# Two head pairs scored in one go, two products with v in one go, and moved buffers, turns and conversions at the two ends of attention

## The chip, the cores and the metric

The kernel runs on one core of a Trainium2 chip. The metric is the time of one execution in microseconds of device time; 561.05 us is the median of three runs of the kernel before (560.88 to 561.12). Engines are named as in the profile: PE is TensorE (PEld its weight loads), DVE is VectorE, ACT is ScalarE, POOL is GpSimd, SP issues most of the DMAs.

## The reference

Three layers follow one another on B = 2 sequences of S = 448 tokens with width C = 768 (12 heads of 64). All is float32.

```python
scores = scale * q @ k.T                      # per head
scores = einsum('bhij,hg->bgij', scores, w_pre)   # heads are mixed before the softmax
attn = softmax(scores, axis=-1)
attn = einsum('bhij,hg->bgij', attn, w_post)      # and after it
x = (attn @ v) as (B, S, 768)
u = x + (relu(x.T @ w_tok1) @ w_tok2).T       # token mixing, 448 -> 256 -> 448
x = u + relu(u @ w_ch1) @ w_ch2               # channel mixing, 768 -> 1536 -> 768
h = gelu(x @ w_in); u, v = halves of h        # 768 -> 2 x 512
v = layernorm(v) * g_ln;  v = w_sg @ v + b_sg # spatial gate over tokens
out = x + (u * v) @ w_out
```

## The kernel before

Nearly every float32 product is computed as three float32r products of split operands (high by high, high by low, low by high); a split is a rounded copy and a subtraction.

**Attention.** A chunk is 120 query rows (88 in the last of a sequence) of all 12 heads; there are eight chunks, four per sequence. `qk` (L345) scores one pair of heads of a chunk: the two heads lie on partitions 0 to 63 and 64 to 127, so each term is two 64-row products into two PSUM banks; two copies bring them to the chunk's tile S. Six pairs make a chunk. A block is 10 query rows by 12 heads, 120 partitions; there are 12 blocks in a full chunk and 9 in a short one, 90 in all. A block's rows are gathered from S by a DMA (`b_dma`, tile P, four buffers in rotation), split by ACT and POOL (`b_high`, `b_low`), mixed over heads and reduced (`b_pre`: three products into a bank of psB, the negated row maximum nm on DVE, the exponential E with its sum on ACT), normalised (`b_norm`: rc, rr on DVE, and wt, the second mixing matrix scaled by the reciprocal sum, on POOL), mixed again and transposed (`b_post`: four products into a bank of psC), and copied to AT by DVE (`b_turn`). `av` (L443) multiplies a finished chunk's AT with v for one pair of heads, in 64-column halves of PE, and copies the result to xT.

The main loop (L544) runs over the steps i from -8 to 89. In step i the DMA of block i+8, the split of i+6, pre of i+4, parts of the normalisation of i+2 and i+1, post of i and the AT copy of i-1 are issued. Every engine works its instructions off in the order written, so this order is the schedule. Extra work hangs on steps: `add(step, fn, ...)` puts it between the normalisation and pre. By it qk of chunk x is spread over the blocks of two chunks before, one pair at a time (L528 to L541), with the splits of the next chunk's q and k (`qprep`, `kprep`: a copy on DVE, a subtraction on POOL) and their loads behind. The products with v of a finished chunk stand in `todo` and are taken one at a time behind post as blocks go by (L575). qk takes two banks of psA, an av one; psA has three banks, psB three, psC two.

**Weights** come as 64-bit floats, and are loaded and converted piece by piece in the order of use: `conv_steps` is a generator, and `pump(n)` takes n calls from it. A piece with a split takes five calls, each of them one DVE instruction or the ACT copy and the subtraction (wl, on POOL for most); `w_abs`, the first step of the next piece (cv, on ACT), is issued at the fourth call; the raw buffers are three, and a finished conversion issues the next load. `rounds(n, w)` advances the evictions that are open and pumps w calls in each of n rounds. Only three converted pieces of the kind in rotation may exist before the first of them is used.

**Behind attention.** `turn` (L462) transposes part of xT back (three PE transposes, then xh on ACT and xl on DVE), since token mixing contracts over tokens: eight turns for the first sequence stand at attention's end, eight for the second within tok1(0), two per group of products. tok1 and tok2 (L653, L673) are the token products; tok2 ends in a chain of an addition on DVE, a copy uh on ACT and a subtraction ul on POOL. The channel products c1 and c2 follow, then the gated layer; there `sps_full(b, d)` (L861) is a quarter of the spatial product of sequence b, followed by the gate's chain (gt twice on DVE, gh on ACT, gl on POOL), and the output products ops read all gates of their sequence.

Of the kernel before, what the change touches and what calls it, by code (L numbers as in the profile page):

```python
# [8 lines left out]
F32 = mybir.dt.float32  # L9
# [10 lines left out]
LD, LS, LP, LN = 8, 6, 4, 2  # L20
NP_BUFS, NPH_BUFS = LD - LS + 2, LS - LP + 1
# [9 lines left out]
def tile_kernel(ctx, tc, q, k, v, w_pre, w_post, w_tok1, w_tok2, w_ch1, w_ch2,  # L31
                w_u, w_v, g_ln, w_sg, b_sg, w_out, out):
    nc = tc.nc
# [63 lines left out]
    def w_dma():  # L97
        i = wstate["dma"]
        if i >= len(pieces):
            return  # L100
        wstate["dma"] += 1
        src, pr, a, n = pieces[i][:4]
        wide = 1 if src.dtype == F32 else 2
        raw = wpool.tile([P, 2 * WC], U32, tag="raw", name=f"raw{i}", bufs=RB)
        r = raw[:pr, :wide * a * n].rearrange("p (a n) -> p a n", a=a)
        nc.sync.dma_start(out=r, in_=src.bitcast(U32))
        wstate["raw"][i] = r
# [64 lines left out]
    def pump(n):  # L172

        for _ in range(n):
            if wstate["conv"] < wstate["room"]:
                next(wstate["steps"], None)
# [107 lines left out]
    def big(nm, dt=F32R):  # L284
        return sp_.tile([P, SWC], dt, tag="S", name=nm, bufs=2)
# [92 lines left out]

    def b_dma(i):
        b, c, j, (r0, stp, m) = blocks[i]  # L380
        t = ap_.tile([BW, S], F32, tag="P", name=f"P{i}", bufs=NP_BUFS)
        nc.sync.dma_start(out=t, in_=SS[b, c][r0:r0 + (m - 1) * stp + 1:stp])
        st[i]["P"] = t

# [39 lines left out]
    def b_post(i):  # L424

        b, c, j, bl = blocks[i]
        if j == 0:
            AT[b, c] = atp.tile([KP, R, H, CH[0][1]], F32, tag="AT", name=f"AT{b}_{c}", bufs=2)
        e, wt = st[i]["e"][0], st[i]["w"]
        ps = psC.tile([P, 512], F32, tag="C", name=f"post{i}")  # L430
        for r in range(R):
            nc.tensor.matmul(ps[:KP, r * BW:(r + 1) * BW], lhsT=e[:, r * KP:(r + 1) * KP], rhs=wt,  # L432
                             start=True, stop=True)
        st[i]["ps"] = ps

    def b_turn(i):

        b, c, j, bl = blocks[i]
        src = st[i]["ps"][:KP, :R * BW].rearrange("p (r g i) -> p r g i", r=R, i=IB)
        nc.vector.tensor_copy(AT[b, c][:, :, :, j * IB:(j + 1) * IB], src)  # L440
        st[i] = None
# [32 lines left out]
    def add(step, fn, *a):  # L474
        extra.setdefault(step, []).append((fn, a))
# [45 lines left out]
    for x in range(2, NCH):  # L521
        b, c = chunks[x]
        n_prev = len(chunk_blocks(CH[chunks[x - 1][1]][1]))
        f0 = first[chunks[x - 1]] - LD
        gap = 3 if n_prev < 12 else 4
        nxt = chunks[x + 1] if x + 1 < NCH else None
        nxt2 = chunks[x + 2] if x + 2 < NCH else None
        for i in range(NP):  # L528
            s_ = f0 + i * n_prev // NP
            LAST = max(LAST, s_)  # L530
            add(s_, qk, b, c, i)
            if nxt and i % QG == QG - 1:
                add(s_ + gap, qprep, *nxt, i // QG)
                if nxt2:
                    add(s_ + gap + 1, load_q, *nxt2, i // QG)
            if nxt and nxt[1] == 0:
                for g, kg in enumerate(KG):
                    if kg[0] == i:
                        add(s_ - 2, load_k, nxt[0], g)

                add(s_ + 2, kprep, nxt[0], i, nc.vector.tensor_copy, nc.gpsimd)  # L541

    todo = []
    for i in range(-LD, NB):  # L544
        if 0 <= i + 1 < NB:
            b_norm(i + 1, 2)
        if i + LD < NB:
            b_dma(i + LD)
        if 0 <= i + LS < NB:
            b_high(i + LS)  # L550
            if i >= 0:
                b_low(i + LS)
        if 0 <= i + LN < NB - (i + LP > NB):
            b_norm(i + LN, 0)
        if i > 0:
            b_turn(i - 1)
        if 0 <= i + LN < NB - (i + LP > NB):
            b_norm(i + LN, 1)
        if i + LP == NB:

            b_norm(NB - 1, 0)
            b_norm(NB - 1, 1)
        for fn, a in extra.get(i, []):
            fn(*a)
        if 0 <= i + LP < NB:
            b_pre(i + LP)
        if -LS <= i < 0:

            b_low(i + LS)
        if i >= 0:  # L570
            b, c, j, bl = blocks[i]
            b_post(i)

            nb = len(chunk_blocks(CH[c][1]))
            while todo and NP - len(todo) < (j + 1) * NP // nb:  # L575
                av(*todo[0])
                if todo[0][1] == len(CH) - 1 and b:
                    add(i + 1, load_v, b, todo[0][2])
                todo.pop(0)
            if j == nb - 1:  # L580
                todo = [(b, c, hp) for hp in range(NP)]
        if i == LAST:
            qctx.close()
            wctx = ctx.enter_context(ExitStack())
            wpool = wctx.enter_context(tc.tile_pool(name="wp", bufs=1, side="right", reuse_waits="tile"))
            tctx = ctx.enter_context(ExitStack())
            tpool = tctx.enter_context(tc.tile_pool(name="tokw", bufs=1, side="right", reuse_waits="tile"))
        if 0 < i - LAST <= 2 * RB and (i - LAST) % 2 == 1:
            w_dma()
        if i + LS + 4 >= NB:  # L590

            pump(1)
    b_turn(NB - 1)

    NS = S // KP
    XR = [big(f"x{nm}0") for nm in "hl"]
    X = {0: [t[:KP, :NS * C].rearrange("p (s c) -> p s c", c=C) for t in XR]}
    RX = {0: [t[:, NS * C:NS * C + TOK // P * C].rearrange("p (t c) -> p t c", c=C) for t in XR]}
    turns = [(0, s, ch) for ch in range(2) for s in range(NS)]

    def turn0(n):
        for _ in range(n):
            turn(psB.tile([P, 512], F32, tag="B", name=f"xps0_{len(turns)}"), *turns.pop(0))

    turn0(3)
    while todo:
        av(*todo.pop(0))
        pump(1)
    turn0(len(turns))
    actx.close()  # L610


# [37 lines left out]
    with ExitStack() as mctx:  # L650
        mp = mctx.enter_context(tc.tile_pool(name="tok", bufs=1, reuse_waits="tile"))
        RR = {}
        def tok1(b, turns=()):  # L653
            xh, xl = X[b]
            t1 = [p for i in p_t1 for p in parts(i)]
            rh, rl = RX[b]
            got = []
            for tt in range(TOK // P):
                ts = slice(tt * P, (tt + 1) * P)
                for ch in range(2):  # L660
                    cs = slice(ch * CW, (ch + 1) * CW)
                    ps = bank(f"t1ps{b}_{tt}_{ch}")
                    mm3(ps[:, :CW], [((t1[s][0][:, ts], t1[s][1][:, ts]), (xh[:, s, cs], xl[:, s, cs]))
                                     for s in range(NS)])
                    got.append(later(relu_split(rh[:, tt, cs], rl[:, tt, cs], ps[:, :CW])))
                    for _ in range(2):
                        if turns:
                            s, tch = turns.pop(0)
                            turn(bank(f"xps1_{s}_{tch}"), 1, s, tch)
                    rounds(2)  # L670
            RR[b] = (rh, rl, got)

        def tok2(b):  # L673
            rh, rl, got = RR[b]
            finish(*got)
            t2 = [p for i in p_t2 for p in parts(i)]
            for cc in range(NCC):
                cs = slice(cc * P, (cc + 1) * P)
                ps = bank(f"t2ps{b}_{cc}")
                mm3(ps[:, :S], [((rh[:, tt, cs], rl[:, tt, cs]), t2[tt]) for tt in range(TOK // P)])  # L680
                U[cc, b] = later(add_split(cc, b, ps[:, :S], uh, ul))
                rounds(1, 1 - b)
                rounds(1, 0)

        X[1] = [mp.tile([KP, NS, C], F32R, name=f"x{nm}1") for nm in "hl"]
        RX[1] = [mp.tile([P, TOK // P, C], F32R, name=f"r{nm}1") for nm in "hl"]
        need(p_t1[-1])

        tok1(0, [(s, ch) for ch in range(2) for s in range(NS)])
        need(p_t2[-1])  # L690
        tok1(1)
        tok2(0)
        tok2(1)
# [167 lines left out]
    def sps_full(b, d):  # L861
        ds = slice(d * P, (d + 1) * P)
        ks = range(MID) if b == 0 else range(MID + 1, NT)
        mm3(banks[b, d][:, :S], [((vh[:, k, ds], vl[:, k, ds]), sg_parts(k, slice(0, P))) for k in ks], start=False)
        G[b, d] = later(gate(b, d, banks[b, d][:, :S]))
        rounds(2)

    finish(*[V[k] for k in range(MID + 1)])
    for d in range(ND - 1):
# [109 lines left out]
```

## Time and profile before

| | |
|---|---|
| median of three runs | 561.05 us |
| the profiled execution's own time | 562.4 us |
| its span in the trace | 560.6 us |
| PE busy | 548.3 us, 98% |
| PEld busy | 476.7 us, 85% |
| DVE busy | 391.6 us, 70% |
| ACT busy | 282.8 us, 50% |
| POOL busy | 282.2 us, 50% |
| granted PE clock, mean of the run | 1.00 |

The busy time of an engine is a union of its instructions' times. PE's products are pipelined: one is shown as running until its last result is out, while the next has begun; what a product costs is therefore read from the distance between two starts and not from its duration. A bracket behind an instruction gives the idle time of its engine before it and what ended it.

### The profile page before, as it was taken

The page shows a single profiled execution, that of the slowest core. Times are in us where ns is not written, and L with a number is a line of the kernel's source. Part 1 is how long each engine was busy: PE and PEld are TensorE (multiplying, and loading weights), DVE is VectorE, ACT ScalarE, POOL GpSimd, SP SyncE. Part 2 cuts the span into 40 slices and gives each one's busy share as a digit, 9 for nine tenths or more (in the row PEclk, how much of TensorE's full clock was granted, in tenths as well). Part 3 has the DMA queues.
Part 4 walks back from the last instruction along what each step waited for, and adds up shares of the span by engine and source line. Part 5 has one row for each costly group of instructions (what it writes and reads, how often), then busy time and mean ns, then how long its engine had stood idle before and what let it go on. Part 6 is the DMA issues. An engine that isn't in the chain of part 4 may idle for free.

```text
span 560.6 us, 10091 instructions
## 1 busy us (share of the span) xinstructions
PE 548.3 (98%) x3630; PEld 476.7 (85%) x3630; DVE 391.6 (70%) x771; ACT 282.8 (50%) x600; POOL 282.2 (50%) x295
## 2 busy tenths in 40 slices
PE   9899999999999999899999999999999999999997
PEld 5677888888888888799789999999999998888786
DVE  4788766555665677778455767678887974795972
ACT  4876776666777665454433344423243343464320
POOL 0599996667666665013922322334544545055610
PEclk9999999999999999999999999999999999999999
DMA  6464534423432362133113443434343323102222
GB/s 203 171 210 136 174 123 99 106 86 121 154 118 87 124 174 50 59 111 115 56 57 94 123 142 112 151 113 151 113 142 121 94 90 111 63 1 68 84 100 98
DMA packets 26340, 63.12 MB, mean 113 GB/s; under 512 B 2914, under 2 KB 18834, under 8 KB 26290
## 3 DMA queue, kind: packets, MB, share of 16 engines
q1 hardware_dynamic: 26002, 62.10, 34.6%
q8 instruction: 29, 0.48, 0.4%
q10 hardware_dynamic: 288, 0.37, 0.2%
q14 instruction: 21, 0.17, 0.1%
HBM read 40.36 MB, written 2.75 MB: 77 GB/s over the span
## 4 chain that ended last, share of the span: by engine, by line
PE 89%; POOL 5%; DVE 3%; ACT 1%; DMA 1%; issue 1%; POOLq 0%; SPq 0%; DVEq 0%; ACTq 0%
PE post L432 13%; PE av L450 7%; PE qk L362 7%; PE c2ps L623 5%; PE c2ps L622 5%; PE c2ps L624 5%; PE c1ps L623 5%; PE c1ps L624 5%; PE pre L399 5%; PE c1ps L622 5%; PE pre L400 3%; PE pre L401 3%; POOL ul L640 3%; PE ups L623 2%; PE ups L624 2%; PE ups L622 2%
## 5 line engine op out<-in xcount | busy, mean ns | idle before, releaser
L393 POOL TENSOR_TENSOR Pl<-P,Ph 120x448 fp32r<-120x448 f32 x87 | 99.5, 1143 | 62.7 <-ACT Ph L387 52.8
L159 POOL TENSOR_TENSOR wl<-cv,wh 128x768 fp32r<-128x768 f32 x28 | 53.0, 1894 | 115.7 <-ACT wh L158 81.2
L432 PEld LDWEIGHTS post<-wt,E 120*112 120x112 f32 x720 | 86.3, 176 | 7.1 <-POOL wt L420 1.7
L432 PE MATMUL post<-wt,E 120*112 120x120 f32 x720 | 88.9, 267 | 1.4 <-POOL wt L420 0.8
L403 DVE TENSOR_REDUCE nm<-pre 120x1 f32<-120x448 f32 x90 | 55.3, 614 | 36.0 <-PE pre L401 35.8
L407 ACT ACTIVATE E<-pre,nm 120x448 f32<-120x448 f32 x90 | 57.3, 636 | 45.3 <-DVE rc L414 31.9
L440 DVE COPY AT<-post 112x480 f32<-112x480 f32 x90 | 58.8, 654 | 7.0 <-PE post L432 0.7
L623 PE MATMUL c1ps<-ul,wh 128*128 128x448 f32 x144 | 53.7, 373 | 1.7 <-POOL ul L640 1.7
L387 ACT CAST Ph<-P 120x448 fp32r<-120x448 f32 x90 | 52.2, 580 | 1.5 <-DMA P<-S 1.5
L623 PE MATMUL c2ps<-r1l,wh 128*128 128x448 f32 x144 | 52.9, 368 | 0.0
L139 DVE SCALAR_TENSOR_TENSOR cv<-raw,cv 128x768 uint32<-128x768 uint32 (+3 forms) x44 | 51.9, 1180 | 1.1
L622 PE MATMUL c1ps<-uh,wh 128*128 128x448 f32 x144 | 52.3, 363 | 0.0
L622 PE MATMUL c2ps<-r1h,wh 128*128 128x448 f32 x144 | 52.3, 363 | 0.0
L624 PE MATMUL c1ps<-uh,wl 128*128 128x448 f32 x144 | 52.0, 361 | 0.0
L624 PE MATMUL c2ps<-r1h,wl 128*128 128x448 f32 x144 | 52.0, 361 | 0.0
L117 ACT ACTIVATE cv<-raw 128x768 f32<-128x768 f32 (+3 forms) x44 | 36.1, 821 | 29.8 <-POOL wl L159 17.6
L365 ACT COPY S<-qk 120x448 f32<-120x448 f32 (+1 forms) x86 | 42.1, 539 | 15.6 <-PE qk L362 13.2
L450 PE MATMUL av<-AT,vn 112*64 112x120 f32 (+1 forms) x768 | 46.5, 266 | 0.4 <-DVE AT L440 0.4
L141 DVE SCALAR_TENSOR_TENSOR cv<-raw,cv 128x768 uint32<-128x768 uint32 (+3 forms) x44 | 42.2, 958 | 1.1
L399 PE MATMUL pre<-Ph,wpl 120*120 120x448 f32 x90 | 40.8, 454 | 1.5 <-DVE rc L414 1.4
L450 PEld LDWEIGHTS av<-AT,vn 112*64 112x64 f32 x768 | 37.0, 137 | 5.6 <-DVE AT L440 0.7
L158 ACT CAST wh<-cv 128x768 fp32r<-128x768 f32 x28 | 23.4, 835 | 31.7 <-DVE cv L141 27.9
(202 smaller groups left out, 1199.9 us busy)
## 6 DMA issues: line engine op xcount, KB each, us to landing
P<-S SPq DMA_DIRECT2D x90, 210.0 KB
raw<-in_w_ch_dram SPq DMA_DIRECT2D x24, 768.0 KB
raw<-in_w_v_dram SPq DMA_DIRECT2D x6, 512.0 KB
raw<-in_w_u_dram SPq DMA_DIRECT2D x4, 768.0 KB
raw<-in_w_out_dram SPq DMA_DIRECT2D x6, 512.0 KB
vn<-in_v_dram SPq DMA_DIRECT2D x12, 224.0 KB
out_dram<-xT SPq DMA_DIRECT2D x12, 224.0 KB
qn<-in_q_dram SPq DMA_DIRECT2D x10, 180.0 KB
```

Source lines behind the costliest of these rows:

```text
L159: nc.gpsimd.tensor_tensor(dst[1], f, f32(dst[0]), op=ALU.subtract)
L387: nc.scalar.copy(hi, st[i]["P"])
L393: eng.tensor_tensor(lo, st[i]["P"], f32(st[i]["h"]), op=ALU.subtract)
L399: nc.tensor.matmul(ps[:BW, :S], lhsT=wpl, rhs=hi, start=True, stop=False)
L403: nc.vector.tensor_reduce(out=nm, in_=ps[:BW, :S], axis=AX.X, op=ALU.max, negate=True)
L407: nc.scalar.activation(e, ps[:BW, :S], AF.Exp, bias=nm, scale=1.0, accum_out=sm)
L432: nc.tensor.matmul(ps[:KP, r * BW:(r + 1) * BW], lhsT=e[:, r * KP:(r + 1) * KP], rhs=wt, start=True, stop=True)
L440: nc.vector.tensor_copy(AT[b, c][:, :, :, j * IB:(j + 1) * IB], src)
L450: nc.tensor.matmul(ps[64 * j:64 * j + 64, :cols], lhsT=vn[b, hp][:, j, r, :], rhs=AT[b, c][:, r, 2 * hp + j, :cols], start=(r == 0), stop= ...
L622: nc.tensor.matmul(ps, lhsT=lh, rhs=rh, start=(start and i == 0), stop=False)
L623: nc.tensor.matmul(ps, lhsT=lh, rhs=rl, start=False, stop=False)
L624: nc.tensor.matmul(ps, lhsT=ll, rhs=rh, start=False, stop=(stop and i == n - 1))
```

## The change

The six qk of a chunk now go two into a step: they stand one behind the other, every fourth block of a full chunk and every third of a short one, the second with one bank of psA and one of psC and its copies on ACT and DVE. The products with v go in pairs as well, at the steps between. The splits and loads that hang on them move by a step or so. P0 and P1 get tiles of their own. All eight turns of the first sequence move into the last four steps of the loop, two per step, and there AT is copied behind its own post. Conversions: two calls and not one behind each of the last six av, two and not one per round in tok1(0), none in tok2(0), and none in sps_full(0, d).

```diff
     def b_dma(i):
         b, c, j, (r0, stp, m) = blocks[i]
-        t = ap_.tile([BW, S], F32, tag="P", name=f"P{i}", bufs=NP_BUFS)
+        if i < 2:
+            t = qp.tile([BW, S], F32, tag=f"P{i}", name=f"P{i}")
+        else:
+            t = ap_.tile([BW, S], F32, tag="P", name=f"P{i}", bufs=NP_BUFS)
...
-        gap = 3 if n_prev < 12 else 4
...
         for i in range(NP):
-            s_ = f0 + i * n_prev // NP
+            s_ = f0 + 1 + i // 2 * n_prev // (NP // 2)
             LAST = max(LAST, s_)
-            add(s_, qk, b, c, i)
+            if i % 2:
+                add(s_, qk, b, c, i, ((psA, "A"), (psC, "C")), (nc.scalar.copy, nc.vector.tensor_copy))
+            else:
+                add(s_, qk, b, c, i)
             if nxt and i % QG == QG - 1:
-                add(s_ + gap, qprep, *nxt, i // QG)
+                add(s_ + 3, qprep, *nxt, i // QG)
                 if nxt2:
-                    add(s_ + gap + 1, load_q, *nxt2, i // QG)
+                    add(s_ + 4, load_q, *nxt2, i // QG)
...
-                add(s_ + 2, kprep, nxt[0], i, nc.vector.tensor_copy, nc.gpsimd)
+                add(s_ + 1 + i % 2, kprep, nxt[0], i, nc.vector.tensor_copy, nc.gpsimd)
...
-        if i > 0:
+        if 0 < i <= NB - LP:
             b_turn(i - 1)
...
             b_post(i)
+            if i >= NB - LP:
+                b_turn(i)
 
             nb = len(chunk_blocks(CH[c][1]))
-            while todo and NP - len(todo) < (j + 1) * NP // nb:
+            while todo and NP - len(todo) < 2 * ((j + nb // 6) * 3 // nb):
                 av(*todo[0])
...
+        if i + LP == NB:
+            XR = [big(f"x{nm}0") for nm in "hl"]
...
+        if i + LP >= NB:
+            for _ in range(2):
+                turn(psB.tile([P, 512], F32, tag="B", name=f"xps0_{len(turns)}"), *turns.pop(0))
         if i + LS + 4 >= NB:
             pump(1)
-    b_turn(NB - 1)
...
-    turn0(3)
     while todo:
         av(*todo.pop(0))
-        pump(1)
-    turn0(len(turns))
+        pump(2)
...
                             turn(bank(f"xps1_{s}_{tch}"), 1, s, tch)
-                    rounds(2)
+                    rounds(2, 2 - b)
...
                 U[cc, b] = later(add_split(cc, b, ps[:, :S], uh, ul))
-                rounds(1, 1 - b)
-                rounds(1, 0)
+                rounds(2, 0)
...
         G[b, d] = later(gate(b, d, banks[b, d][:, :S]))
-        rounds(2)
+        rounds(2, b)
```

## Rows read from the trace of the kernel before

**Rows 1.** Windows: us, then each engine's busy us, clock, DMA share, GB/s

```profile
22.00:84.00 62.00, 61.22 (x506) 49.68 (x506) 48.67 (x130) 46.16 (x118) 59.14 (x75) 1.00 0.49 160
84.00:222.00 138.00, 138.00 (x1280) 116.54 (x1281) 88.11 (x265) 93.36 (x239) 91.51 (x123) 1.00 0.36 111
```

**Rows 2.** Timeline of PE: a qk alone, an av alone (start, duration, what)

```profile
101.94 0.47 PE L362 MATMUL qk<-KH,QH 64*120 64x448 f32 x2
...
102.75 0.46 PE L399 MATMUL pre<-Ph,wpl 120*120 120x448 f32 x1
...
103.46 0.98 PE L432 MATMUL post<-wt,E 120*112 120x120 f32 x8
104.37 1.04 PE L450 MATMUL av<-AT,vn 112*64 112x120 f32 x16
105.34 0.47 PE L399 MATMUL pre<-Ph,wpl 120*120 120x448 f32 x1
```

**Rows 3.** Timeline of PE: av and qk joined, then a plain block

```profile
160.40 1.04 PE L450 MATMUL av<-AT,vn 112*64 112x120 f32 x16
...
162.18 0.46 PE L399 MATMUL pre<-Ph,wpl 120*120 120x448 f32 x1
...
162.89 0.98 PE L432 MATMUL post<-wt,E 120*112 120x120 f32 x8
163.64 0.44 PE L399 MATMUL pre<-Ph,wpl 120*120 120x448 f32 x1
```

**Rows 4.** Timeline of PE: sps_mid of three d in a row

```profile
508.07 0.58 PE L859 MATMUL sps<-w,vh 64*128 64x448 f32 x4
...
508.68 0.57 PE L859 MATMUL sps<-w,vh 64*128 64x448 f32 x4
```

**Rows 5.** Timeline of PE: an av of 90 columns alone

```profile
132.63 0.84 PE L450 MATMUL av<-AT,vn 112*64 112x90 f32 x16
133.40 0.47 PE L362 MATMUL qk<-KH,QH 64*120 64x448 f32 x2
```

**Rows 6.** Timeline of PE: two waits of the tail, six av

```profile
225.42 1.05 PE L432 MATMUL post<-wt,E 120*112 120x120 f32 x8 [0.64 <-DVE AT L440]
...
230.96 3.94 PE L450 MATMUL av<-AT,vn 112*64 112x90 f32 x96 [0.43 <-DVE AT L440]
```

**Rows 7.** Timeline of POOL at the ramp

```profile
21.54 1.14 POOL L393 TENSOR_TENSOR Pl<-P,Ph 120x448 fp32r<-120x448 f32 x1 [1.99 <-DMA P<-S]
```

**Rows 8.** Groups of DVE instructions, 237 to 257 us: busy, mean ns, idle before

```profile
L470 DVE TENSOR_TENSOR xl<-xps,xh 112x384 fp32r<-112x384 f32 x11 | 5.7, 552 | 3.6 <-ACT xh L469 3.5
```

**Rows 9.** Timeline of DVE: the last xl pair, conversion calls of wide pieces

```profile
248.82 1.02 DVE L470 TENSOR_TENSOR xl<-xps,xh 112x384 fp32r<-112x384 f32 x2
...
251.72 0.55 DVE L137 TENSOR_SCALAR cv<-cv 128x768 uint32<-128x768 uint32 x1
252.30 0.96 DVE L139 SCALAR_TENSOR_TENSOR cv<-raw,cv 128x768 uint32<-128x768 uint32 x1
...
262.89 2.23 DVE L137 TENSOR_SCALAR cv<-cv 128x768 uint32<-128x768 uint32 x1
```

**Rows 10.** Timeline of PE: second group of tok1(1), its third token tile

```profile
251.58 0.34 PE L622 MATMUL t1ps<-xh,t_2h 112*128 112x384 f32 x1
```

**Rows 11.** Timeline of PE: the first products of c1

```profile
274.33 0.37 PE L622 MATMUL c1ps<-uh,wh 128*128 128x448 f32 x1
...
282.13 0.36 PE L622 MATMUL c1ps<-uh,wh 128*128 128x448 f32 x1
...
282.74 0.36 PE L622 MATMUL c1ps<-uh,wh 128*128 128x448 f32 x1
```

**Rows 12.** Timeline of ACT: a conversion among the gates

```profile
517.59 0.67 ACT L117 ACTIVATE cv<-raw 128x512 f32<-128x512 f32 x1 [4.12 <-DMA raw<-in_w_out_dram]
```

**Rows 13.** Timeline of PE: the first output products, 37th at the end

```profile
525.11 0.36 PE L622 MATMUL ops<-gh,wh 128*128 128x448 f32 x1
...
535.05 0.36 PE L622 MATMUL ops<-gh,wh 128*128 128x448 f32 x1
```

More of the change, by code (lines that the diff above doesn't have):

```diff
@@ L539, in tile_kernel @@
                         add(s_ - 2, load_k, nxt[0], g)
-                add(s_ + 2, kprep, nxt[0], i, nc.vector.tensor_copy, nc.gpsimd)
+                add(s_ + 1 + i % 2, kprep, nxt[0], i, nc.vector.tensor_copy, nc.gpsimd)
     todo = []
+    NS = S // KP
+    X, RX = {}, {}
+    turns = [(0, s, ch) for ch in range(2) for s in range(NS)]
     for i in range(-LD, NB):
@@ L589, in tile_kernel @@
             w_dma()
+        if i + LP == NB:
+            XR = [big(f"x{nm}0") for nm in "hl"]
+            X[0] = [t[:KP, :NS * C].rearrange("p (s c) -> p s c", c=C) for t in XR]
+            RX[0] = [t[:, NS * C:NS * C + TOK // P * C].rearrange("p (t c) -> p t c", c=C) for t in XR]
+        if i + LP >= NB:
+            for _ in range(2):
+                turn(psB.tile([P, 512], F32, tag="B", name=f"xps0_{len(turns)}"), *turns.pop(0))
         if i + LS + 4 >= NB:
             pump(1)
-    b_turn(NB - 1)
[L595 to L603, printed above, removed]
-    turn0(3)
     while todo:
         av(*todo.pop(0))
-        pump(1)
-    turn0(len(turns))
+        pump(2)
     actx.close()
```

## The prediction

> **What bounds the kernel now.** Two stretches of the table of windows say where time can be had [rows 1]. From 84 to 222 us, the steady part of attention, TensorE (PE) is busy 138.00 of 138.00 us while GpSimd (POOL), the next, has 91.51: there a saved PE microsecond is a saved microsecond, as long as no shorter cover breaks. From 22 to 84 us PE is busy 61.22 of 62.00, but POOL has 59.14: two engines share the bound, and the change takes nothing off POOL. Then I read PE's timeline for what a detour costs; the reader is to look at distances between starts, since busy times overlap. Last come the waits PE does have: a tail at the end of attention [rows 6], the start of the first channel product [rows 11], the start of the last product [rows 13].
>
> **Products with v and scores.** A plain block goes from post to the next pre in 0.75 us (162.89 to 163.64) and from pre to post in 0.71 [rows 3]. A qk alone takes 0.81 to the pre behind it; post to av takes 0.91 and av to pre 0.97 [rows 2]. So leaving the plain chain costs 0.91 - 0.75 = 0.16, and a detour costs 0.16 + 0.81 = 0.97 with one qk, 0.16 + 0.97 = 1.13 with one av. An av with a qk behind it takes 1.78 to pre [rows 3], both prices with the 0.16 paid once: a joined av and qk is 0.16 cheaper than two detours.
>
> The price of a second one. For qk, no two split-term qk follow each other, but sps_mid has its shape (three rounds of two 64-row products of 448 columns): one inside a run takes 0.61 (508.07 to 508.68) [rows 4]. For av, the last six stand in a row: with 90 columns one alone lasts 0.84 and takes 0.77 to its successor [rows 5], six last 3.94 [rows 6], so a further one takes (3.94 - 0.84) / 5 = 0.62, 0.15 less. I take the same 0.15 at 120 columns: 0.82. A pair of qk then costs 0.16 + 0.81 + 0.61 = 1.58, saving 2 x 0.97 - 1.58 = 0.36; a pair of av costs 0.16 + 0.97 + 0.82 = 1.95, saving 2 x 1.13 - 1.95 = 0.31. If a second one is no cheaper, only 0.16 is left in each.
>
> The count, from the loop. Of 36 qk in the loop (chunks 2 to 7) 26 have an av directly before them now; afterwards there are 18 pairs, and two of them stand behind a pair of av. So 24 joins are lost, 0.16 each. From step 28 on (84 us): 12 qk pairs x 0.36 = 4.3, 15 av pairs x 0.31 = 4.6, less 17 joins x 0.16 = 2.7: **6.2 us** gained (bounds 3.0, where seconds cost most, to 7).
>
> Does cover hold? The second qk puts one product in a bank of psC and copies it on VectorE (DVE). The next post takes the other psC bank and waits for the AT copy of the post before it; that copy has both qk (1.4 us) and a pre in front of the deadline. The post after that waits for the DVE copy. It starts 0.71 + 0.75 + 0.68 = 2.1 us after the pair ends, and the copy needs about 0.65 (an estimate: L470's 0.552 for 384 columns [rows 8], scaled to 448). Behind the copy on DVE stands nm, which needs that pre anyway. Cost nothing; 1.4 us is the slack. Two plain blocks in a row leave POOL and DVE little room, but POOL's share there is two thirds [rows 1] and its tiles are made a block or two ahead.
>
> **22 to 84 us and the ramp.** By the same prices steps 4 to 28 save 6 x 0.36 + 4 x 0.31 - 7 x 0.16 = 2.3. POOL is idle for 62.00 - 59.14 = 2.9 us there [rows 1], partly because its inputs come late, and the conversions of k are pushed into neighbouring steps. I count 1.0 of the 2.3 (0 to 2.3). The moves around it I cost at nothing: load_k keeps its step, while kprep comes up to a block (0.71 + 0.75 us) earlier, so a late k transfer would hold DVE with nm queued behind KH, three times 1.5 us at most, which the lower end holds; qprep and load_q shift by a block and stay four steps ahead of their qk; LAST falls a step earlier, and with it the first three w_dma in SP's queue, ahead of P transfers that have two blocks to spare. At the ramp P0 and P1 get tiles of their own, so the DMAs of P4 and P5 no longer wait for tile readers in SP's queue, where everything behind them waits too. POOL's idle 1.99 us before 21.54 ended with such a DMA [rows 7]. It goes; next late is the POOL chain itself. I count 1.2 (0 to 2.0). Together **2.2**.
>
> **The tail.** All eight turns move to the last four blocks, two each, between posts: the same PE work, put where pre has ended, and AT is copied right behind its post. PE's waits of 0.64 (post, for DVE's AT) and 0.43 (av) [rows 6] go; two more av pairs save 0.15 each. **1.4** (0.3 to 2). New there: two xl and a conversion call per block on DVE; PE feels their lateness only once the third psB bank behind a turn is not free, and a post in between gives DVE 1 us each.
>
> **Conversions ahead of the token products.** Calls go from 10 + 6 to 10 + 12 by the end of attention, then from 2 to 4 per group in tok1(0), and to none in tok2(0). Four pairs of DVE's xl in tok1(0) feed tok1(1). The last pair ended at 248.82 + 1.02 = 249.84 [rows 9]; PE first needs it at 251.75, one product behind 251.58 [rows 10]: 1.9 us of slack, and DVE had 3.5 us of waits for ACT's xh [rows 8]. Before that pair now stand twelve calls, not six, and wide ones: three without DVE, five at 0.55 and four at 0.96 [rows 9], 6.6 us, against 2.3 for six narrow ones (an estimate by columns, 448 for 768). That adds 4.3; the longer queue from the av loop leaves some 1.3 more. So the pair comes 4.3 + 1.3 - 3.5 - 1.9 = 0.2 us late if nothing stretches. A DVE call beside a POOL wl took 2.23 instead of 0.55 [rows 9]; two wl stand in front of the pair: up to 2 x 1.7 = 3.4 more. I take **-1.5** (0 to -3.8). The Trainium skill (GPSIMD Engine Reference, Specifications) says that GpSimd shares its SBUF interfaces with VectorE and contends with instructions in a two-port mode or with two SBUF inputs. By that rule every one of these conversions is exposed and the term is nearer -3.5 (a sum of 11.9); the 2.23 row agrees for one of them.
>
> What it buys: c1 lost time where PE waited for ul. Seven triples took 282.13 - 274.33 = 7.80, where a triple takes 0.61 (282.13 to 282.74) [rows 11]: 7.80 - 4.27 = 3.5 lost. In front of POOL's ul and DVE's adds stood wl and its conversion calls; they are gone from tok2(0). I take **3.2** (1.0 to 3.5).
>
> **The last stage.** sps_full(0, d) pumps nothing now. Before, ACT sat 4.12 us in cv for a w_out DMA [rows 12], and gh stands behind it in ACT's queue, so the gates of b = 0 came late. From 525.11 to 535.05 PE ran 12 triples [rows 13]: 9.94 - 7.32 = 2.6 lost. The calls now stand among the gates of b = 1, which are needed only 5 us after the first output product begins; five calls are all there is room for. **2.4** (1.0 to 2.6).
>
> **Sum.** 6.2 + 2.2 + 1.4 - 1.5 + 3.2 + 2.4 = 13.9. Against the profiled execution's 562.4 (span 560.6 and 1.8 around it) that gives 548.5; the runs' median is 561.05, 1.35 lower, so 547.2.
>
> **Rivals.**
> 1. POOL keeps the front. For it: 59.14 of 62.00 [rows 1]; against: 1.99 us of its idleness go [rows 7]. The 2.2 fall away: 11.7 gained, 549.4.
> 2. The conversions collide. tok1(1) waits 3.8, and ul, just as late as PE, still holds c1: the terms -1.5 and 3.2 become -3.8 and 0, 8.4 gained, 552.7. For it the 2.23 row, against it the idle 3.5 us.
> 3. The price is per product and not per change of shape, so pairing doesn't do what it says. From step 28: 12 x 0.16 + 15 x 0.16 - 2.7 = 1.6 instead of 6.2; 9.3 gained, 551.8. Rows 4 and 6 speak against it, though both are of other products.
> 4. Slower: post waits for psC. The DVE copy of a second qk stands behind AT and a conversion of k or q, and post waits for its bank in each of 18 pairs. From 1.4 us of lateness on it costs PE; from 1.4 + 13.9 / 18 = 2.2 us in every pair the kernel is slower. At 2.4 us: 18 x 1.0 - 13.9 = 4.1 lost, 565.2. For it: DVE is in-order and takes on 18 copies; against: PE never waits from 84 to 222, and DVE has 50 us free there (88.11 of 138) [rows 1].
>
> **How the numbers follow.** Forecast 0.55, rivals 0.18, 0.15, 0.07 and 0.05. Gains and losses within 0.2% (1.1 us), about what a measurement of this kernel can tell from no change, need most terms to fail at once: 0.02, taken from rivals 2 and 3. Slower 0.04 from rival 4, the rest of it ending as a small gain; faster 0.94. Low end 541.5: steady 7, front 4.3, tail 2, tok1 0, c1 3.5, last 2.6 make 19.4. High end 554.5: past rivals 1 to 3 alone, with two of them partly together. The forecast's own range is 543 to 550.
>
> **What would show it.** Right: a second qk begins 0.71 behind the first and ends 0.61 later; a second av 0.82 to 0.85; from step 28 to the last pre PE has no wait. POOL's first long idle at 20 us shrinks. c1's first triples run at 0.61 each, as do those of the last product. tok1(1)'s second group shows one wait for xl, 0 to 4 us. Wrong: post waiting for DVE's S copy, or for wt in steps 18 to 28; PE waiting at xl for more than 4 us; ul still the chain's end behind tok2.

## The result and the profile after

The changed kernel takes **553.06 us** (median of four runs, 552.82 to 555.51) against 561.09 us for the kernel before in the same comparison: 0.9868 of its time, with a 95% interval of 0.9853 to 0.9882, 8.0 us less. The forecast was 547.2 in a range of 541.5 to 554.5: the sign was right and the time lies in the range, but 5.9 us of the forecast gain did not come.

The profiled execution took 552.82 us (span 550.9), 0.24 below its median, where that of before lies 1.35 above its own. The two traces therefore differ by 9.7 us and not by 8.0, and it is these 9.7 that the marks below divide. The page of the changed kernel, the same two windows as in [rows 1], then PE's longest waits (the column after the colon: us in total, times, longest):

```profile
span 550.9 us, 10089 instructions
...
PE 537.3 (98%) x3630; PEld 477.5 (87%) x3630; DVE 394.8 (72%) x789; ACT 274.0 (50%) x582; POOL 280.8 (51%) x295
```

```profile
22.00:84.00 62.00, 60.35 (x514) 50.95 (x514) 48.30 (x140) 42.30 (x109) 59.59 (x74) 1.00 0.48 158
84.00:222.00 138.00, 137.11 (x1351) 121.60 (x1349) 96.86 (x287) 90.42 (x236) 90.90 (x124) 1.00 0.37 114
```

```profile
PE t1ps L629 <- ACT xT L462: 2.5, 1, 2.5
PE t1ps L629 <- ACT xh L473: 1.8, 1, 1.8
PE post L436 <- POOL wt L424: 1.5, 2, 1.2
```

PE is still busy for 98%. Of these rows of before's list of waits, the first two are gone:

```profile
PE c1ps L623 <- POOL ul L640: 1.7, 7, 0.3
PE ops L623 <- POOL gl L837: 1.4, 2, 1.2
PE post L432 <- POOL wt L420: 0.8, 1, 0.8
```

Two long waits are new, both of the token product for ACT. Cut at the first start of a stage on PE, the stages compare so; a stage runs from the mark named to the next:

| from | before, at | lasts | after, at | lasts | gained | forecast |
|---|---|---|---|---|---|---|
| start | 0 | 15.01 | 0 | 14.89 | 0.1 | |
| first pre | 15.01 | 6.95 | 14.89 | 5.96 | 1.0 | 1.2 |
| post of block 0 | 21.96 | 197.88 | 20.85 | 190.66 | 7.2 | 1.0 + 6.2 |
| post of block 85 | 219.84 | 17.46 | 211.51 | 18.93 | -1.5 | 1.4 |
| t1ps (tok1, tok2) | 237.30 | 33.99 | 230.44 | 36.50 | -2.5 | -1.5 |
| c1ps | 271.29 | 90.92 | 266.94 | 87.36 | 3.6 | 3.2 |
| c2ps, ups, vps, sps | 362.21 | 162.90 | 354.30 | 162.90 | 0.0 | 0 |
| ops, 36 products | 525.11 | 9.94 | 517.20 | 7.69 | 2.2 | 2.4 |
| 37th, to the end | 535.05 | 25.5 | 524.89 | 26.0 | -0.5 | 0 |

**Where it came from.** PE's timeline of a pair of qk and a pair of av, to be read start to start as [rows 2, 3] were:

```profile
83.23 0.47 PE L362 MATMUL qk<-KH,QH 64*120 64x448 f32 x2
...
83.94 0.37 PE L362 MATMUL qk<-KH,QH 64*120 64x448 f32 x2
...
84.63 0.46 PE L403 MATMUL pre<-Ph,wpl 120*120 120x448 f32 x1
...
87.68 1.86 PE L454 MATMUL av<-AT,vn 112*64 112x120 f32 x32
89.47 0.47 PE L403 MATMUL pre<-Ph,wpl 120*120 120x448 f32 x1
```

The second qk begins 0.71 behind the first and the pair takes 1.40 to pre (forecast 0.81 + 0.61 = 1.42); the pair of av takes 1.79 (forecast 0.97 + 0.82). The first products of c1 and of ops, which correspond to [rows 11] and [rows 13]:

```profile
266.94 0.37 PE L629 MATMUL c1ps<-uh,wh 128*128 128x448 f32 x1
...
271.19 0.36 PE L629 MATMUL c1ps<-uh,wh 128*128 128x448 f32 x1
```

```profile
517.20 0.36 PE L629 MATMUL ops<-gh,wh 128*128 128x448 f32 x1
...
523.88 0.36 PE L629 MATMUL ops<-gh,wh 128*128 128x448 f32 x1
524.89 0.36 PE L629 MATMUL ops<-gh,wh 128*128 128x448 f32 x1
```

Seven triples of c1 take 4.25 us where they took 7.80. In ops one triple of twelve still loses 0.4 (1.01 between the last two rows, for 0.61).

**Where it went.** The end of attention on PE, and the same stretch on ACT:

```profile
226.43 1.46 PE L454 MATMUL av<-AT,vn 112*64 112x90 f32 x32 [0.31 <-DVE xT L462]
230.44 0.45 PE L629 MATMUL t1ps<-xh,t_0h 112*128 112x384 f32 x1 [2.55 <-ACT xT L462]
```

```profile
229.62 0.56 ACT L158 CAST t_0h<-cv 128x448 fp32r<-128x448 f32 x1 [1.52 <-DVE cv L141]
230.09 0.29 ACT L459 COPY xT<-av 128x80 f32<-128x80 f32 x1
230.21 0.18 ACT L462 COPY xT<-av 128x8 f32<-128x8 f32 x1
```

The last copies of av to xT stand in ACT's queue behind a conversion's cast t_0h, and that cast waits 1.52 us for DVE, which is still on the calls before it. By the code, the attention's banks are closed in front of the first token product, which takes its own from the same memory: it waits for these copies, and PE stands still for 2.55 us. Within tok1(1) the same happens again; PE, then ACT:

```profile
246.71 0.45 PE L629 MATMUL t1ps<-xh,t_2h 112*128 112x384 f32 x1 [1.80 <-ACT xh L473]
```

```profile
245.06 0.83 ACT L158 CAST wh<-cv 128x768 fp32r<-128x768 f32 x1 [1.29 <-DVE cv L141]
245.80 0.48 ACT L650 ACTIVATE xh<-t1ps 128x384 fp32r<-128x384 f32 x1
246.18 0.85 ACT L473 CAST xh<-xps 112x384 fp32r<-112x384 f32 x2
```

The turns' xh stands behind the cast wh, which waits 1.29 us for DVE's cv.

### The profile page after: what moved, and what is told of

Same layout as the page of the kernel before. It is cut to its first block, busy times and chain, and to the rows that moved or that the text cites. A ratio compares the mean times of both kernels' runs of the same rounds, so it can differ in the third digit from the quotient of the medians.

```text
span 550.9 us, 10089 instructions
## 1 busy us (share of the span) xinstructions
PE 537.3 (98%) x3630; PEld 477.5 (87%) x3630; DVE 394.8 (72%) x789; ACT 274.0 (50%) x582; POOL 280.8 (51%) x295
## 4 chain that ended last, share of the span: by engine, by line
PE 85%; DVE 6%; issue 2%; POOL 2%; ACT 2%; DMA 1%; SPq 0%; POOLq 0%; ACTq 0%
PE post L436 11%; PE av L454 7%; PE qk L362 5%; PE c1ps L630 5%; PE c2ps L630 5%; PE c2ps L629 5%; PE c1ps L629 5%; PE c2ps L631 5%; PE c1ps L631 5%; PE pre L403 4%; PE pre L405 3%; PE pre L404 3%; PE ups L629 2%; PE ups L631 2%; PE ups L630 2%
## 5 line engine op out<-in xcount | busy, mean ns | idle before, releaser
L454 PE MATMUL av<-AT,vn 112*64 112x120 f32 (+1 forms) x768 | 42.0, 263 | 0.3 <-DVE xT L462 0.3
L454 PEld LDWEIGHTS av<-AT,vn 112*64 112x64 f32 x768 | 37.1, 137 | 3.1 <-PE av L454 0.5
L652 DVE SCALAR_TENSOR_TENSOR r1l<-c1ps,r1h 128x448 fp32r<-128x448 f32 x24 | 15.0, 624 | 31.2 <-ACT r1h L650 31.2
```

What stands on the lines that cost most here:

```text
L454: nc.tensor.matmul(ps[64 * j:64 * j + 64, :cols], lhsT=vn[b, hp][:, j, r, :], rhs=AT[b, c][:, r, 2 * hp + j, :cols], start=(r == 0), stop= ...
```

## Experiments

Theory: the pairs, the ramp, c1 and ops bring what was forecast, and the missing 5.9 us are the two new waits, each of which comes from one place where two conversion calls are issued instead of one. Rivals: a wait that is taken away comes back at the next place; the conversions taken away there are missing later, in c1 or ops; or the pairs bring less than the marks say. "After" and "before" name the kernel that an experiment is made from.

**1 to 3. One call instead of two, at either place and at both.** a_loop1 is after with the first edit, b_tok1 with the second, c_both with both.

```diff
     while todo:
         av(*todo.pop(0))
-        pump(2)
+        pump(1)
...
-                    rounds(2, 2 - b)
+                    rounds(2)
```

> The changed kernel with one conversion call, not two, behind each of the last six av. Theory: the first token product waits 2.55 us because ACT's cast t_0h, which waits for DVE's conversion, stands in ACT's queue ahead of the last av's copy; with six calls fewer there the wait falls below 0.6 us and the kernel to about 551 us. Rival: the wait comes from the turns and AT copies moved into the last four blocks; then it stays, and the time stays at 553 us.

> The changed kernel with one call and not two per round in tok1(0). Theory: the wait in tok1(1) for the turned rows (2.3 us) goes, and c1 stays free of waits for ul since tok2(0) still issues no call: about 550.8 us. Rival: c1 lost its waits only because PE arrives later by the waits before it; then they come back by 2 us or so, and the time stays within 1 us of 553.

> The changed kernel with both edits: one call behind each of the last av and one per round in tok1(0). Theory: both waits go and c1 stays free: 548.5 us. Rival: the 14 calls now missing before c1 make PE wait there for its weights, some 3 us: 551 us or more.

a_loop1 took 551.48 us (551.37 to 551.64; 0.982 of before, 0.9804 to 0.9837), b_tok1 551.83 (551.3 to 552.65; 0.9828, 0.9812 to 0.9844), c_both **546.82** (546.7 to 547.1; 0.9738, 0.9723 to 0.9753), 1.7 below what its theory expected. Each edit takes away its wait and no other. In c_both both are gone, c1's ul did not come back, and the stage from block 85 to t1ps lasts 16.29 us, that from t1ps to c1ps 34.03: 2.64 and 2.47 less than after, 5.1 of the 6.0 to 6.2 us by which the medians differ (after was not timed beside c_both; counted from the kernel before timed with each, the difference is 6.5 and, for k_both2 below, 5.8). PE in c_both, where the av meets the first token product:

```profile
225.62 1.46 PE L454 MATMUL av<-AT,vn 112*64 112x90 f32 x32 [0.31 <-DVE xT L462]
227.01 0.44 PE L629 MATMUL t1ps<-xh,t_0h 112*128 112x384 f32 x1
```

The rivals of a wait that comes back and of conversions missing later fall: c1 to c2 takes 87.36 as in after. But singly the edits brought 1.6 and 1.2 us, together 6.2. The profiles of the single ones show why. In each the wait that is left is followed by a stretch at a lower granted clock (last but two in a row: the clock). b_tok1 behind its 2.55 us wait for xT, then a_loop1 behind its 1.92 us wait for xh, each with the row of the wait ahead:

```profile
229.52 0.69 PE L629 MATMUL t1ps<-xh,t_0h 112*128 112x384 f32 x1 [2.55 <-ACT xT L462]
...
228.00:230.00 2.00, 0.48 (x1) 0.48 (x2) 1.97 (x8) 0.77 (x3) 0.66 (x1) 0.82 0.58 171
230.00:232.00 2.00, 2.00 (x8) 2.00 (x8) 1.58 (x2) 0.92 (x1) 0.48 (x1) 0.50 0.89 326
232.00:234.00 2.00, 2.00 (x9) 1.89 (x8) 0.00 (x0) 0.24 (x1) 0.00 (x0) 0.50 0.77 192
234.00:236.00 2.00, 2.00 (x9) 2.00 (x8) 1.00 (x2) 1.67 (x4) 0.00 (x0) 0.50 0.57 240
236.00:238.00 2.00, 2.00 (x14) 1.96 (x14) 1.63 (x3) 0.31 (x1) 1.15 (x1) 0.97 0.00 0
```

```profile
244.00 0.45 PE L629 MATMUL t1ps<-xh,t_2h 112*128 112x384 f32 x1 [1.92 <-ACT xh L473]
...
244.00:246.00 2.00, 1.85 (x7) 1.58 (x8) 1.97 (x5) 1.22 (x3) 1.09 (x1) 0.80 0.84 332
246.00:248.00 2.00, 2.00 (x8) 2.00 (x7) 1.93 (x3) 0.42 (x2) 0.00 (x0) 0.50 0.00 0
248.00:250.00 2.00, 2.00 (x12) 2.00 (x11) 1.64 (x4) 1.45 (x3) 0.53 (x1) 0.85 0.32 52
```

Eight or nine products in 2 us, where 14 stand at full clock: 0.50 is the lower of the two levels. In b_tok1 t1ps to c1ps takes 37.1 us although no wait is left there, 3.1 more than in c_both. The medians of the single edits contain such stretches: the mean clock is 0.993 to 0.997 in all eight of their runs, where c_both has 0.999 or 1.000. That the wait brings the lower clock about is not shown (see the last section).

**4 to 6. The pairs alone, and one kind of pair alone.** d_pairs is before with the pairing of qk and of av (the hunks of `add(s_, qk, ...)`, with the shifts of the splits and loads that hang on it, and of `while todo`) and nothing else; e_qk has the first hunk only, f_av the second.

```diff
+            s_ = f0 + 1 + i // 2 * n_prev // (NP // 2)
...
+            while todo and NP - len(todo) < 2 * ((j + nb // 6) * 3 // nb):
```

> The kernel before with the pairs of qk and of av alone (and the shifts of kprep, qprep, load_q that hang on them). Theory: a detour of PE costs 0.16 us once, a second qk 0.61 and not 0.81, a second av 0.82 and not 0.97: 7 us less than before, about 554 us, of which 6 from block 28 on. Rival, price per product: about 558 to 560 us.

> The kernel before with pairs of qk alone; av stay single. Theory (a detour costs 0.16 us once, joins counted): 18 pairs save 0.36 each, but nearly all of the 26 joins of av and qk are lost, 0.16 each: about 2.3 us less, 559 us, far under half of what both kinds of pairs gave together. Rival, each kind of pair saves by itself what it saves in the changed kernel: about 3 to 4 us less, 557.5 us, and the two alone add up to the whole.

> The kernel before with pairs of av alone; qk stay single. Theory: 21 pairs save 0.31 each, the 26 joins go at 0.16 each: about 2.3 us less, 559 us. Rival: about 3 us or more less, and with the pairs of qk alone the sum is that of both together.

d_pairs: 555.24 us (554.8 to 555.53; 0.9887, 0.9872 to 0.9901), 6.1 less than before. e_qk: 561.23 (0.9996, 0.9987 to 1.0005), nothing. f_av: 559.68 (0.9972, 0.996 to 0.9984), 1.6 less. Both together bring far more than the sum of each, and the timelines say why by a count of the detours from the chain of pre and post: before has 55, because 26 of its qk stand directly behind an av; with qk paired alone there are 60, with av paired alone 56, with both 40. Pairing one kind breaks the joins with the other, 0.16 each, and gains only its own seconds. In e_qk the front takes part of that back: from the post of block 28 to that of block 85 it takes 133.83 where before takes 134.46, with one more qk in it, a gain of 1.4 to 1.6; but in front of block 28 its post waits 1.5 us for wt, where f_av, g_ramp, h_sps and i_tok2 have 0.5 to 0.6. These waits come with the pairs of qk. From the post of block 0 to t1ps, d_pairs takes 208.47, f_av 212.99 and e_qk 214.09 us, where h_sps, i_tok2 and g_ramp below, which have before's code there, take 214.88 to 214.95: 6.4, 1.9 and 0.8 less. e_qk's median shows none of its 0.8 (its interval reaches to 0.7), and its expectation missed by 2.2. d_pairs' trace keeps before's waits for ul and gl, and its stage from block 85 to t1ps lasts 17.58, before's 17.46: the tail is not the pairs' doing.

**7 and 8. The late moves alone.** h_sps is before with `rounds(2, b)` in sps_full, i_tok2 with `rounds(2, 0)` in tok2.

```diff
-        rounds(2)
+        rounds(2, b)
...
-                rounds(1, 1 - b)
-                rounds(1, 0)
+                rounds(2, 0)
```

> The kernel before with no conversion call in sps_full(0, d). Theory: the gates of the first sequence are not held by ACT's wait for a weight transfer, the first 12 triples of the output product lose 0.3 us instead of 2.6: 2.2 us less than before, about 558.9 us. Rival: the calls moved among the gates of the second sequence hold those instead; then the loss moves to the third and fourth output product and the time stays within 1 us of before.

> The kernel before with no conversion call in tok2(0), and nothing moved ahead in its place. Theory: ul is no longer late, the first c1 products lose nothing instead of 3.5 us: about 557.6 us. Rival: the calls have to be made up ahead of their use, and PE waits for weights in the first c1 or c2 products: within 1.5 us of before.

h_sps: 558.91 us (0.996, 0.9947 to 0.9973); its first 36 products of ops take 7.92 us where before took 9.94. i_tok2: 557.5 (0.9937, 0.9921 to 0.9954); its first seven triples of c1 take 4.25 for 7.80, and t1ps to c1ps 33.99, as before. So the calls taken out of tok2(0) need not be issued earlier at all: nothing later went short of them here. That settles what the double calls of after were worth: they make room for this move, but the move did not need it.

**9. The ramp alone.** g_ramp is before with tiles of their own for P0 and P1.

> This is the kernel before with the P tiles of the first two blocks in buffers of their own, and nothing else of the change. Theory (the wait of 1.2 us of the ramp goes, and the front behind it keeps its pace): pre(0) to post(0) falls from 6.95 to about 5.96 us and the time from 561.1 to 560.1. Rival (the front is bound by POOL, which gives the time back in later waits of post for wt): post(0) earlier by 1.0 but post(28) at the old distance from the start, and the time 561.1.

560.41 us (0.9987, 0.9977 to 0.9997), 0.5 less than before. First pre to post of block 0 takes 5.96 for 6.95, and block 28 comes 1.4 earlier than in before's trace. The theory's 1.0 lies in the interval (0.2 to 1.3 us), the rival's zero just outside.

**10. More joins.** j_join is c_both with the av at other blocks, so that pairs of qk stand behind av; c_both was timed again beside it (k_both2).

```diff
-            while todo and NP - len(todo) < 2 * ((j + nb // 6) * 3 // nb):
+            while todo and NP - len(todo) < 2 * ((j + nb // 3) * 3 // nb):
```

> This is c_both with the av products of a block taken up in pairs at three other places of the block's work, so that about 12 of the qk pairs stand directly behind a pair of av and share one detour with it instead of making one of their own. Theory (the price of a detour's two switches is 0.16 us and is saved once for each join): 12 x 0.16 = 1.9 us less than c_both, 546.8 - 1.9 = 544.9 us; post(0) to post(85) on TensorE falls from 190.7 to about 188.8, and nothing else moves. Rival (detours that are twice as long, followed by more plain blocks in a row, starve DVE's and POOL's preparation of the next post): the waits of post for wt, rr or AT grow by as much as the joins save, and the time is 546.5 to 548.

> c_both once more, on the same chip as j_join, so that the two can be compared: 546.8 us (546.5 to 547.2), with post(0) to post(85) at 190.7.

j_join took 547.49 us (546.89 to 548.5), c_both this time 547.08 (546.79 to 547.5): no gain, as the rival had it. Twelve joins are there where after has two, but from the post of block 0 to t1ps it takes 207.12 us against 207.01. Its waits, against 1.5 in c_both for the first row and no such second row:

```profile
PE post L436 <- POOL wt L424: 3.1, 5, 1.2
...
PE av L454 <- DVE AT L444: 0.8, 1, 0.8
```

Ten more joins at 0.16 are 1.6; the two rows have grown by 1.6 + 0.8. The five waits for wt all lie between 36 and 84 us. POOL is busy 57.47 us from 22 to 84 us in j_join and 59.59 of 62.00 in after, so its sum alone does not explain them; that it is the longer rows of plain blocks that bring POOL late is argued, as in the rival, and not tried by itself.

## Why the prediction held, and where it failed

- **Steady part, 6.2: right.** From the post of block 28 to that of block 85 it takes 134.46 before and 129.19 after (5.3 less), and the part after has one more qk in it, 0.8 to 0.97: 6.1 to 6.2. The price per detour, 0.16, rests on start distances and on the lost joins of runs 5 and 6. The Trainium skill (TensorEngine Tiling (Array Packing), Key Properties) says that a change of tiling mode drains TensorE. The trace agrees in kind: the 0.16 us of a detour are paid when 64-row or 64-column products follow full ones.
- **Front, 1.0, and ramp, 1.2: 1.0 and 1.0 in the profiled pair.** The DMA wait of [rows 7] is gone (POOL's split there now starts at 20.44, behind ACT). But before's profiled execution is 0.45 us longer between blocks 0 and 28 than those of h_sps, i_tok2 and g_ramp, which have the same code there (63.42 against 62.96 to 63.02): the front is worth nearer 0.5 (62.97 - 61.47, less 0.97 for a qk that before does in front of block 28 and after behind it). Rival 1, POOL keeps the front, was half right: 1.5 us of waits for wt stand there, 0.8 before, and e_qk shows that they come with the pairs of qk.
- **Tail, 1.4: the step that failed, -1.5.** The paragraph counted PE's waits for AT, which did go, and with one call per av (c_both) the stage gains 17.46 - 16.29 = 1.2, near the forecast. It put no price on the two calls behind each of the last six av. These calls appear only in the paragraph on the conversions, and there only as a queue on DVE. What they do is put an ACT cast with a wait for DVE in front of ACT's copy of the last av: 2.55 us, on the path.
- **Token products, -1.5: -2.5, right product, wrong queue.** The wait stands at the t_2h product that was named, but for ACT's xh (1.80 us); the xl that DVE makes from it holds the product behind by another 0.4 (it starts 0.59 later, in c_both 0.18). The working followed only DVE's queue and overlooked that every fifth call is a cast on ACT that waits for it. Rival 2 (waits of 3.8 and ul still in c1) fell with ul. The Trainium skill (GPSIMD Engine Reference, Specifications) says that GpSimd shares its SBUF interfaces with VectorE and contends with DVE instructions in a two-port mode or with two SBUF inputs. The trace agrees for the first of the two DVE calls below, which reads two SBUF tiles; in which mode the second runs it does not show. Beside a POOL subtraction they took 1.44 and 1.05 us, where calls of the same form with none beside them took 0.63 and 0.55 (DVE, then POOL):

```profile
228.21 0.63 DVE L139 SCALAR_TENSOR_TENSOR cv<-raw,cv 128x448 uint32<-128x448 uint32 x1
...
230.45 1.44 DVE L139 SCALAR_TENSOR_TENSOR cv<-raw,cv 128x448 uint32<-128x448 uint32 x1
...
235.12 1.05 DVE L135 TENSOR_SCALAR cv<-cv 128x768 f32<-128x768 f32 x1
...
239.95 0.55 DVE L135 TENSOR_SCALAR cv<-cv 128x768 f32<-128x768 f32 x1
```

```profile
230.26 1.16 POOL L159 TENSOR_TENSOR t_0l<-cv,t_0h 128x448 fp32r<-128x448 f32 x1 [15.02 <-ACT t_0h L158]
234.61 1.15 POOL L159 TENSOR_TENSOR t_1l<-cv,t_1h 128x448 fp32r<-128x448 f32 x1 [3.19 <-ACT t_1h L158]
```

The calls right in front of the wait (0.95, 0.96 and 0.55 us) have no POOL instruction beside them, so they test nothing. What the two long ones add to the 1.80 us is not shown. The -3.5 that the prediction set beside this term did not come.

- **c1, 3.2: 3.6. Last stage, 2.4: 2.2.** Both by the mechanism named, and each holds by itself (runs 7 and 8). The 0.5 lost at the very end is not the last stage's: it lies behind PE's last product, and e_qk and d_pairs, which have before's code there, take 26.03 us from the 37th product on as well, h_sps 25.56. What makes it is open.
- **Rivals 3 and 4** fell: pairs bring 6.1 us by themselves, and no wait of post for psC stands in the list.
- **The sum.** With the tail and the token products as they came, the terms give 13.9 - 2.9 - 1.0 = 10.0, beside 9.7 in the traces. The measured 553.06 lies in the range of 541.5 to 554.5, but above the 543 to 550 that the prediction called the forecast's own, and the range held because it was wide enough for the rivals. That it lies beside rival 2's 552.7 is chance: of that rival's two terms, -3.8 and 0, the measured ones are -2.5 and 3.6. c_both, without the double calls, takes 546.8 to 547.1, close to the 547.2 that was forecast, and this is in part chance too: it loses nothing in the token products (34.03 us, before 33.99), where the forecast held -1.5, and its front gains less than the 1.0.

Left open: what moves the start. c_both is another 1 us below after beyond the 5.1 us of its two stages, and between the two profiled executions 0.85 of it lies in front of the first pre (14.89 and 14.04 us), where the two kernels have the same code; over all thirteen profiles that start lies between 13.93 and 15.28. In k_both2, the same kernel as c_both, it is 14.98, and the execution is 5.3 us shorter than after's. Two of after's four runs also had a mean clock of 0.993 and 0.996 (555.51 and 553.22 us), the others 0.999, so its median may hold a little of the lower clock.

## What to carry to other kernels

When filler work is put into gaps, follow it through every engine's queue that it enters, not only through the one that does most of it: a cast that waits for another engine, ahead of the copy that frees a bank, stops the bottleneck engine even where all engines have time to spare. Price detours by start distances and count them: pairing one kind of detour can be worth nothing as long as it parts it from another kind that it was joined with. And try a removal alone before adding work elsewhere to make up for it: here the calls taken out of tok2(0) were missed nowhere.

## What was not expected of the hardware

In two kernels a single PE wait of about 2 us was followed by a stretch at the lower clock. After the 2.55 us in b_tok1 the clock was 0.50 until about 236 us, after the 1.92 us in a_loop1 until about 249; in after's profiled execution, with both waits (2.55 and 1.80 us), it stayed at 1.00. So it is not every time. Over whole runs the mean clock was 0.996 or 0.997 in all four of a_loop1 and 0.993 to 0.996 in all four of b_tok1, and 0.999 or 1.000 in all eight of c_both, which has neither wait. That the wait is the cause was not tried by itself; g_ramp, without such a wait, also had two runs of ten at 0.996 (561.38 and 561.33 us, its slowest), and the kernel before, without one too, a run at 0.996 and one at 0.997 (562.64 and 562.55 us).
